# Two fp32 tiles instead of three in a fused attention and FFN kernel, with a new emission order

## The chip, the cores and the metric

One core of a Trainium2 chip runs the whole program. The metric is the device time of one execution in microseconds. A profiled execution gives the trace from which the rows below are read.

## The reference

Attention with rotary position embedding over 4 batches, 8 heads, 576 positions and head size 64, followed by a feed-forward network (FFN) without biases; both keep the accuracy of fp32.

```python
q_rot, k_rot = rotate(q), rotate(k)              # 4 x 8 x 576 x 64
scores = q_rot @ k_rot^T / sqrt(64)
attn = softmax(scores)
x = (attn @ v) as 2304 tokens x 512
h = x @ w_in                                     # 512 x 2048
g = h * clip(h + 3, 0, 6) / 6
out = g @ w_out                                  # 2048 x 512
```

The weights come as 64-bit floats and are decoded on the chip.

## The kernel before

The 2304 tokens are 18 tiles of 128. Attention works by head: 18 x 8 heads, numbered `i`, tile `t = i // 8`. Tiles 0 and 1 have an attention of their own in fp32 (`scores_first`, `attention_first`, `emit_first`), since nothing is ready yet; the others use fp16 halves: a value is a high fp16 part and a low fp16 part (`split_steps`), and a product is a sum of several fp16 products. For a later head, `attention(i)` runs the scores on TensorE (4 matmuls of 288 columns, L641), maximum and exponential on VectorE and ScalarE (L689, L692), the split of the result (L706, L710), a transposing DMA (L716), and the product with V on TensorE (14 matmuls of 64 columns, L659).

The FFN of a tile has four blocks of 512 hidden values. `ffn_h` makes `h`, `gate` the activation, `ffn_o` the output. The first `NF` (for `h`: `NH`) tiles, 0, 1 and 2, go in fp32: 64 matmuls of 128 columns (L994) and 16 of 512 columns (L1072). Each of them shows in the trace as two records. The other tiles take three fp16 products: 192 matmuls of 128 columns (L1005) and 48 of 512 columns (L1076). Their x is split in halves and transposed by DMA (`emit_x`, L942 to L950); that of tile 2 is transposed on TensorE (`emit_x32`, L906, through L356), as it is used in fp32. Their gate ends with a copy to fp16 and a subtraction (L1038 to L1040).

Each weight comes in eight pieces. `load_w` issues the loads on SyncE's queue, `decode_w` makes fp32 of them (ScalarE, then VectorE, L588), `bound_w` takes the largest absolute value (`wb` is its priority; `em.choose("wb" + kind, ...)` picks VectorE or ScalarE), `scale_w` makes one scale per weight when its eight bounds are there (`wscale`), and `split_w_steps` splits a piece in place into fp16 halves. It may do so when all fp32 tiles have used the piece (`used_h`, `used`), all 16 pieces are decoded and the scale is there.

The order of the instructions on every engine is the result of a small event simulation in the kernel (class `Emission`): a task is a generator that asks for an engine and a duration, has a priority, and is emitted when the modelled engine is free. `CFG` holds the priorities, and biases by which `choose` prices one engine against another for a kind of work: the key is the kind and the engine's letter (`wboD` is a bound of w_out on VectorE, `loD` a low half on VectorE, `hiP` a high half on GpSimd). There is a phase for the time until both scales are there, one until w_out is split, and a steady one after that; the first list of biases is that of the first phase. `lead` says how far attention may run ahead of the FFN.

Of the kernel before, what the change touches and what calls it, by code (L numbers as in the profile page):

```python
# [10 lines left out]
F16 = mybir.dt.float16  # L11
# [17 lines left out]
NG = 9  # L29
NP16 = 5  # L30
NR1 = 2
NF = 3
NH = 3
NQ = 1
NPT = 4


CFG = {'a0': -1.043, 'a1': -3.605, 'a2': 0.974, 'k1': -29.702, 'kv': 1.769, 'q1': 7.56, 'q': -6.449, 'wi': 8.789, 'wo': 8.272, 'gate': -5.153, 'x': -17.664, 'lead': 16, 'lat': 0.008, 'dma': 2.513, 'back': 0.938, 'a16': -1, 'v0': 1.625, 'wb': 8.917, 'si': 39.868, 'so': 46.239, 'bias': [{'loD': -32.8, 'elD': -3.19, 'glD': -43.45, 'ehD': 9.44, 'ghD': -8.07, 'ropeD': 22.52, 'xhD': -22.31, 'xlD': 3.83, 'hiP': -12.11, 'ehP': -11.5, 'ghP': 46.76, 'xhP': -6.78, 'lowP': 43.5, 'sgP': 45.86, 'hiD': -5.54, 'wboD': -25.15, 'qbD': 19.8, 'biD': -12.43, 'lowD': 31.78, 'sgD': 25.7, 'mxA': 35.95, 'wbiD': -40.0}, {'loD': -6.35, 'elD': 32.31, 'glD': 28.97, 'ehD': 2.19, 'ghD': 20.72, 'ropeD': -5.14, 'xhD': 15.28, 'xlD': 10.72, 'hiP': 46.71, 'ehP': 35.11, 'ghP': -0.16, 'xhP': -16.14, 'lowP': -7.78, 'sgP': 5.66, 'hiD': 14.24, 'wboD': 17.36, 'qbD': 17.86, 'biD': 17.27, 'lowD': 27.25, 'sgD': 34.77, 'mxA': 49.38, 'wbiD': -45.6}, {'loD': -12.12, 'elD': -8.64, 'glD': 11.8, 'ehD': 6.42, 'ghD': 1.59, 'ropeD': 4.05, 'xhD': -14.03, 'xlD': -21.15, 'hiP': 29.79, 'ehP': -7.99, 'ghP': -38.73, 'xhP': -6.56, 'lowP': 12.34, 'sgP': -25.71, 'hiD': 7.07, 'wboD': -25.64, 'qbD': 13.79, 'biD': 3.66, 'mxA': 56.44, 'wbiD': -44.43}], 'kvs': 4, 'vpos': 1, 'q0': 'DP', 'ch': 9.975, 'ks': 4.636, 'h': 9.28, 'r1': 'P', 'late': 2.97, 'r1n': 8, 'steady': {'x': -16.457, 'lead': 36, 'a2': -1.508, 'gate': -14.915, 'kv': 21.843, 'q': -15.069, 'dma': 0.74}, 'swap': -99.0}


class Emission:
# [36 lines left out]
    def free(self, name):  # L78
        self.tokens[name] += 1
# [31 lines left out]
    def step(self, gen, prio, end, prev, sent=None):  # L111

        try:
            e, x = gen.send(sent)
        except StopIteration:
            return
        if prev == "E" and e != "E":
            end += 0.17
        go = lambda t, p=None, s=None: self.post(t, lambda: self.step(gen, prio, t, p, s))
        if e == "N":  # L120
            go(end, prev)
        elif e == "U":
            go(end + x)
        elif e == "T":
            if x["done"]:
                go(end)
            else:
                x["then"].append(lambda t: self.step(gen, prio, max(t, end), None))
        elif e in "SZ":
            self.post(end + 0.05, lambda: self.dma(x, e, lambda t: self.step(gen, prio, t + (CFG["steady"] if self.phase == 2 else CFG)["dma"], None)))  # L130
        elif e == "C":
            self.post(end, lambda: self.poll(x, gen, prio, None))
        elif e == "R":
            def take():
# [27 lines left out]
    def choose(self, kind, x, prio):  # L162

        def cost(e):
            E = e.upper()
            ahead = max(self.busy[E] - self.clock, 0.0) + sum(w[2] for w in self.waiting[E] if w[0] <= prio)
            if e in "dP":
                ahead = max(ahead, self.port - self.clock - self.PORT[E])
            return ahead + x[e] + CFG["bias"][self.phase].get(kind + E, 0.0)
        return min(x, key=cost)  # L170

    def dispatch(self, e):
# [17 lines left out]
def attention_ffn(ctx: ExitStack, tc, q, k, v, w_in, w_out, rope, ident, out):  # L190
# [10 lines left out]
    em = Emission({"S": 2, "P16": NP16, "PT": NPT, "av": 1, "x": 1, "h": 2, "tg": 2, "g": NG,  # L201
                   "o": 1, "ob": 1, "rope": 1, "rope0": 1, "k16": 1, "raw": 3, "raw1": NR1, "tw": 2, "rope1": 1})
    free, when, spawn = em.free, em.when, em.spawn
    cfg = lambda k: (CFG["steady"] if em.phase == 2 else CFG)[k]

    left = ctx.enter_context(tc.tile_pool(name="left", bufs=1))
    psum = ctx.enter_context(tc.tile_pool(name="psum", bufs=1, space=bass.MemoryType.PSUM))
# [64 lines left out]
    tw_free = [0, 1]  # L272
# [101 lines left out]
    def prep_q(t, raw):  # L374

        x, at = raw
        yield "T", at
        am = col("qam", 1, 2)
        e = yield "Xqb", {"D": 0.675, "A": 0.72}
        q1 = left.tile([128, 8, 2, 64], F16, tag="q16", bufs=2, name="q1")  # L380
        bound(e, am, x, q1.rearrange("p h a d -> p (h a d)")[:, 0:512])
        yield "D", 0.54
        p2 = pow2_rows(am, "qp2", 2, 2.0 ** -14)
        s = col("qs", 1, 2)
        DVE.reciprocal(out=s, in_=p2)
# [12 lines left out]
        SP.dma_start_transpose(out=qT[:, 1], in_=q2.rearrange("p h a d -> p (h a d)"))
        yield "P", 0.65
        pk = p2k[b0] if b0 == b1 else mixcol(p2k[b0], p2k[b1], f"pkm{t}")  # L400
        sg = col("sig", 2, 3)
        POOL.tensor_tensor(out=sg[:, 0:1], in0=p2, in1=pk, op=ALU.mult)
        POOL.tensor_scalar(out=sg[:, 1:2], in0=sg[:, 0:1], scalar1=2.0 ** -17, scalar2=None, op0=ALU.mult)
        POOL.tensor_scalar(out=sg[:, 0:1], in0=sg[:, 0:1], scalar1=-2.0 ** -17, scalar2=None, op0=ALU.mult)
        sig_t[t] = sg
        yield "N", 0.0
        if em.phase == 2:
            yield "U", CFG["late"]
        qT_t[t] = qT


# [151 lines left out]
    def decode_w(kind, i, raw, at, token):  # L563

        yield "T", at

        yield "C", lambda: kind == "i" or len(k32_in) == 5 and 0 in qT_t

        yield "C", lambda: kind == "i" or i < 6 or len(tw) == 4
        c = stage(kind, i)  # L570

        yield "A", 1.15
        ACT.activation(out=c, in_=raw[:, :, 1].bitcast(F32), func=ACTF.Prelu, scale=2.0 ** -112, alpha=-2.0 ** 32)
        yield "R", "tw"
# [12 lines left out]
        yield "d", 1.21
        DVE.scalar_tensor_tensor(out=cu, in0=cu, scalar=3, in1=low,  # L588
                                 op0=ALU.logical_shift_left, op1=ALU.bitwise_or)
        yield "N", 0.0  # L590
        decoded[kind].add(i)

        def give():
            tw_free.append(n)
            free("tw")

        spawn(bound_w(kind, i, t, give), CFG["wb"])
        spawn(split_w_steps(kind, i), CFG["s" + kind] + i / 1000)

    def bound_w(kind, i, t, give):  # L600
        c = stage(kind, i)
        e = em.choose("wb" + kind, {"D": 1.21, "A": 1.16}, 3)
        if e == "D":
            give()
        yield e, 1.21 if e == "D" else 1.16
        bound(e, wam[kind][:, i:i + 1], c, t.bitcast(F16)[:, 0:1024])
        yield "N", 0.0
        if e == "A":
            give()
        bounded[kind].add(i)  # L610

    def split_w_steps(kind, i):

        yield "C", lambda: min(used_h, default=8) > i - 2 if kind == "i" else min(used, default=8) > i
        yield "C", lambda: decs() == 16 and kind in wscale and set(range(i - 1 if kind == "i" else i)) <= split_w[kind]
        if kind == "i":
            c, hi, lo = stage(kind, i), wi_h(i, 0), wi_h(i, 1)
        else:
# [51 lines left out]
    def attention(i):  # L670
# [462 lines left out]
    kv = []  # L1133
# [103 lines left out]
```

## Time and profile before

| | us |
|---|---|
| median of 3 runs | 606.47 |
| lowest, highest | 606.04, 609.99 |
| the profiled execution | 608.99 |
| its span | 607.1 |
| TensorE busy | 576.2 |
| VectorE busy | 457.6 |
| ScalarE busy | 354.5 |
| GpSimd busy | 290.6 |

The profile calls TensorE's matmuls PE and its weight loads PEld, VectorE DVE, ScalarE ACT, GpSimd POOL and SyncE's queue SPq. L12 is line 12 of the kernel. A matmul is drawn from its start to the end of its result, so that successive ones overlap; the step from one start to the next is what it costs in a stream. The granted TensorE clock is the full 2.4 GHz nearly throughout (0.996 of it as a mean).

### The profile page before, as it was taken

What the parts mean: (1) busy time and instruction counts of PE and PEld (TensorE: products, weight loads), DVE (VectorE), ACT (ScalarE), POOL (GpSimd) and SP (SyncE); (2) the same over time, 40 slices, a digit from 0 to 9 for tenths busy, and PEclk for the clock granted to TensorE, in tenths of its full rate; (3) what the DMA queues carried; (4) which work ended last, traced back from release to release, by engine and by line L of the source; (5) the groups of instructions that cost most, each with busy time, mean ns of one, the idle gap of its engine ahead of it and who ended that gap; (6) DMA issues with size and microseconds to landing.
All of it is one profiled execution on the core that took longest, in us unless ns stands there. A gap on an engine that the chain in (4) does not pass through costs nothing.

```text
span 607.1 us, 17399 instructions
## 1 busy us (share of the span) xinstructions
PE 576.2 (95%) x7153; PEld 437.6 (72%) x7153; DVE 457.6 (75%) x850; ACT 354.5 (58%) x660; POOL 290.6 (48%) x373
## 2 busy tenths in 40 slices
PE   3888999999999998999999999999999999999996
PEld 2667777767667776787777777867677778777785
DVE  5998999996999985689588859877794877742131
ACT  5797875346777655476556545847564756541111
POOL 5540685423226995446299744545153643223200
PEclk9998999999999999999999999999999999999999
DMA  8989991996669969888986899899969798760000
GB/s 300 304 275 295 277 231 52 143 171 175 123 134 185 140 124 159 207 130 161 183 175 139 156 169 198 148 160 159 149 108 170 129 151 146 135 105 18 19 18 18
DMA packets 240287, 94.71 MB, mean 156 GB/s; under 512 B 222160, under 2 KB 224592, under 8 KB 240208
## 3 DMA queue, kind: packets, MB, share of 16 engines
q1 hardware_dynamic: 240208, 93.60, 76.8%
q8 instruction: 56, 0.92, 0.6%
q14 instruction: 23, 0.19, 0.1%
HBM read 31.97 MB, written 4.72 MB: 60 GB/s over the span
## 4 chain that ended last, share of the span: by engine, by line
PE 60%; DVE 15%; POOL 12%; DMA 6%; issue 5%; ACT 2%; SPq 0%; DVEq 0%; ACTq 0%; POOLq 0%
PE h L1005 17%; PE o L1076 17%; PE o L1072 6%; PE av L659 6%; PE S L641 5%; PE h L994 4%; POOL kst L316 3%; POOL ropeA L313 3%; DVE S L689 2%; POOL kst L318 2%; DMA wi_st<-x 2%; DMA PT<-P 2%; DVE P L710 2%; PE S L644 2%; POOL g L1040 1%
## 5 line engine op out<-in xcount | busy, mean ns | idle before, releaser
L1005 PEld LDWEIGHTS <-wi_st 128*128 128x128 f16 x2880 | 176.1, 98 | 41.9 <-issue 2.7
L1076 PE MATMUL o<-wo_st,g 128*128 128x512 f16 (+1 forms) x636 | 161.5, 367 | 3.7 <-POOL g L1040 2.0
L692 ACT ACTIVATE S<-S,mx 128x576 f32<-128x576 f32 x128 | 91.4, 714 | 114.3 <-DVE S L689 101.9
L689 DVE TENSOR_SCALAR_CACHE_REDUCE S<-S,sig 128x576 f32<-128x576 f32 x128 | 103.4, 819 | 20.1 <-PE S L641 19.2
L1005 PE MATMUL h<-wi_st 128*128 128x128 f16 x1728 | 116.8, 219 | 1.2 <-DMA wi_st<-x 1.2
L710 DVE SCALAR_TENSOR_TENSOR P<-S,P 128x576 f16<-128x576 f32 x128 | 95.1, 753 | 27.8 <-ACT P L706 27.3
L330 POOL TENSOR_SCALAR g<-tg 128x512 f16<-128x512 f32 x45 | 29.2, 649 | 153.5 <-DVE tg L1029 147.7
L1022 ACT ACTIVATE tg<-h,g,block_sc 128x512 f32<-128x512 f32 x64 | 49.7, 776 | 65.5 <-PE h L1005 61.9
L1029 DVE SCALAR_TENSOR_TENSOR tg<-tg,h 128x512 f32<-128x512 f32 x60 | 41.0, 684 | 57.0 <-ACT tg L1022 56.9
L706 ACT ACTIVATE P<-S 128x576 f16<-128x576 f32 x128 | 81.7, 649 | 2.4 <-DMA PT<-P 0.3
L659 PEld LDWEIGHTS <-PT 128*128 128x128 f16 (+1 forms) x2016 | 67.4, 101 | 17.4 <-issue 5.5
L1076 PEld LDWEIGHTS <-g 128*128 128x128 f16 x636 | 54.5, 98 | 31.7 <-issue 3.0
L1005 PE MATMUL h<-xTa,wi_st 128*128 128x128 f16 x1152 | 77.1, 219 | 0.0
L659 PE MATMUL av<-vA,PT 128*128 128x64 f16 (+1 forms) x2016 | 73.0, 194 | 1.0 <-DMA PT<-P 0.6
L641 PE MATMUL S<-kT,qT 128*128 128x288 f16 x448 | 71.2, 286 | 2.1 <-DVE P L710 1.8
L1040 POOL TENSOR_TENSOR g<-tg,g 128x512 f16<-128x512 f32 x47 | 57.9, 1233 | 2.9
L994 PEld LDWEIGHTS h<-xTa,wi_st 128*128 128x128 f32 x384 | 48.1, 192 | 13.7 <-issue 12.8
L641 PEld LDWEIGHTS <-qT 128*128 128x128 f16 x448 | 39.5, 98 | 18.5 <-issue 5.0
L1072 PE MATMUL o<-wo_st,g 128*128 128x512 f32 x96 | 51.0, 613 | 0.7 <-DVE wo_st L588 0.7
L994 PE MATMUL h<-xTa,wi_st 128*128 128x128 f32 x384 | 49.2, 275 | 0.0
L313 POOL TENSOR_TENSOR ropeA<-qraw,rope_sb 128x512 f32<-128x512 f32 x17 | 23.8, 1401 | 33.5 <-DMA qraw<-in_q 33.4
L1076 PE MATMUL o<-wo_st 128*128 128x512 f16 (+1 forms) x132 | 32.4, 360 | 1.4 <-DVE wo_st L328 1.1
(151 smaller groups left out, 760.6 us busy)
## 6 DMA issues: line engine op xcount, KB each, us to landing
raw<-in_w_in SPq DMA_DIRECT2D x16, 512.0 KB, 6.6
raw<-in_w_out SPq DMA_DIRECT2D x16, 512.0 KB, 5.7
qraw<-in_q SPq DMA_DIRECT2D x18, 256.0 KB, 3.8
kst<-in_k SPq DMA_DIRECT2D x16, 256.0 KB, 4.8
vst<-in_v SPq DMA_DIRECT2D x15, 256.0 KB, 4.7
out<-wo_st SPq DMA_DIRECT2D x14, 256.0 KB, 3.5
PT<-P SPq DMA_TRANSPOSE x128, 3.4
vA<-vA SPq DMA_DIRECT2D x8, 256.0 KB, 4.2
```

What stands on the lines that cost most here:

```text
L641: PE.matmul(out=S[:, j, 0:288], lhsT=qT_t[t][:, o, h, :], rhs=kT_t[b0][:, h, ks], **st)
L659: PE.matmul(out=av[r0:r1, h, :], lhsT=PT[:, blk, r0:r1], rhs=rhs, start=(n == 0), stop=(n == len(terms) - 1))
L689: DVE.tensor_scalar(out=E, in0=E, scalar1=sig_t[t][:, 0:1], scalar2=3.0e38, op0=ALU.mult, op1=ALU.min, accum_out=mx)
L692: ACT.activation(out=E, in_=E, func=ACTF.Exp, scale=-1.0, bias=mx, accum_out=sum_t[t][:, h:h + 1])
L706: ACT.activation(out=hi, in_=E, func=ACTF.Copy, scale=ES)
L710: DVE.scalar_tensor_tensor(out=lo, in0=E, scalar=ES, in1=hi, op0=ALU.mult, op1=ALU.subtract)
L994: PE.matmul(out=h[:, i, :], lhsT=wi_st[:, p + 2, 256 * c + f0:256 * c + f0 + 128], rhs=xT[:, c, :], start=(c == 0), stop=(c == 3))
L1005: PE.matmul(out=h[:, i, :], lhsT=wi_h(p, wl)[:, 256 * c + f0:256 * c + f0 + 128], rhs=xT[:, 4 * xl + c, :], start=(n == 0), stop=(n == 11))
L1022: ACT.activation(out=tg, in_=hf, func=ACTF.Relu, scale=osc[j], bias=g3)
L1040: ENG[e].tensor_tensor(out=gf[:, 1], in0=tg, in1=gf[:, 0], op=ALU.subtract)
L1072: PE.matmul(out=os[n][0], lhsT=g[:, mm % nm, 128 * n:128 * n + 128], rhs=wo_st[:, mm + 2], start=(mm == 0), stop=(mm == 15))
L1076: PE.matmul(out=os[n][0][:, to], lhsT=g[:, gl, mm % nm, 128 * n:128 * n + 128], rhs=wo_h(mm, wl)[:, cs], start=(mm == 0 and gl == 0 and wl ...
```

## The change

Tile 2 goes through the FFN in fp16 halves like the later ones (`NF` and `NH` from 3 to 2). The planner's constants are new throughout. In the steady phase there are four sets of them, with biases of their own, chosen by the number of heads that are done (`PARTS`: up to 64, 88, 112 and above). Only two pieces of w_in, not all eight, are loaded into the two early buffers (`r1n`), the others into the three of w_out, and the pool of the FFN's tiles takes the place of the early buffers as soon as these are free. A bound on ScalarE takes a scratch tile of its own in place of keeping that of the decoding. The split of a piece waits for the scales of both weights.

```diff
-NF = 3
-NH = 3
+NF = 2
+NH = 2
+PARTS = 64, 88, 112
-CFG = {... 'wi': 8.789, 'wo': 8.272, 'lead': 16, 'wb': 8.917, 'bias': [{... 'wboD': -25.15, ... 'wbiD': -40.0}, ...
+CFG = {... 'wi': 10.746, 'wo': 3.955, 'lead': 22, 'wb': 12.863, 'bias': [{... 'wboD': 39.4, ... 'wbiD': -1.83}, ...
-  'vpos': 1, ... 'r1n': 8, 'steady': {'x': -16.457, 'lead': 36, ...}, 'swap': -99.0}
+  'vpos': 3, ... 'r1n': 2, 'steady': [{'x': -11.166, 'lead': 38, ... 'bias': {...}}, {... 'lead': 22, ...}, {... 'lead': 16, ...}, {... 'lead': 28, ...}], 'swap': -77.644, 'wbn': 1}
...
-            return ahead + x[e] + CFG["bias"][self.phase].get(kind + E, 0.0)
+            return ahead + x[e] + self.bias().get(kind + E, 0.0)
...
-    cfg = lambda k: (CFG["steady"] if em.phase == 2 else CFG)[k]
+    em.now = lambda: CFG["steady"][bisect.bisect_right(PARTS, len(done_av))] if em.phase == 2 else CFG
+    em.bias = lambda: em.now()["bias"] if em.phase == 2 else CFG["bias"][em.phase]
+    cfg = lambda k: em.now()[k]
...
-        spawn(bound_w(kind, i, t, give), CFG["wb"])
+        tw_free.append(n)
+        free("tw")
+        spawn(bound_w(kind, i), CFG["wb"])
         spawn(split_w_steps(kind, i), CFG["s" + kind] + i / 1000)
...
+    def bound_w(kind, i):
+        yield "C", lambda: decs() >= CFG["wbn"]
+        c = stage(kind, i)
+        e = em.choose("wb" + kind, {"D": 1.21, "A": 1.16}, 3)
+        if e == "A":
+            yield "R", "tw"
+            n = tw_free.pop()
...
-        yield "C", lambda: decs() == 16 and kind in wscale and set(range(i - 1 if kind == "i" else i)) <= split_w[kind]
+        yield "C", lambda: decs() == 16 and len(wscale) == 2 and set(range(i - 1 if kind == "i" else i)) <= split_w[kind]
```

The two waits of the steady phase that were `CFG["late"]`, and the model's delay behind a DMA, are taken from the set of the part.

## Rows read from the trace of the kernel before

**Rows 1.** The page's head and part 1: busy us, share, instructions.
```profile
span 607.1 us, 17399 instructions
PE 576.2 (95%) x7153; PEld 437.6 (72%) x7153; DVE 457.6 (75%) x850; ACT 354.5 (58%) x660; POOL 290.6 (48%) x373
```

**Rows 2.** By stretch: length, busy us (instructions) PE, PEld, DVE, ACT, POOL, clock, DMA, GB/s.
```profile
0.00:50.00 50.00, 32.56 (x265) 24.75 (x266) 43.09 (x70) 36.86 (x66) 22.42 (x24) 0.99 0.98 294
50.00:200.00 150.00, 147.91 (x1500) 110.23 (x1499) 137.58 (x235) 100.83 (x172) 68.83 (x80) 0.99 0.79 174
200.00:550.00 350.00, 344.34 (x4798) 262.24 (x4794) 265.54 (x530) 207.34 (x410) 188.73 (x258) 1.00 0.86 151
...
100.00:130.00 30.00, 29.58 (x292) 21.58 (x292) 29.60 (x55) 12.75 (x28) 10.95 (x16) 1.00 0.85 156
130.00:175.00 45.00, 45.00 (x357) 31.10 (x354) 37.17 (x64) 29.76 (x49) 8.22 (x13) 1.00 0.63 140
```

**Rows 3.** TensorE's timeline from 301 us: start, length, line, matmuls.
```profile
301.39 0.57 PE L659 MATMUL av<-vA,PT 128*128 128x64 f16 x14
301.80 0.65 PE L641 MATMUL S<-kT,qT 128*128 128x288 f16 x4
302.29 0.81 PE L1076 MATMUL o<-wo_st,g 128*128 128x512 f16 x3
302.94 0.83 PE L1005 MATMUL h<-wi_st 128*128 128x128 f16 x12
303.61 0.81 PE L1076 MATMUL o<-wo_st,g 128*128 128x512 f16 x3
```

**Rows 4.** The chain that ended last, in order of time: start, us, records.
```profile
54.86 0.89 PE h L994 x8
...
64.95 0.86 PE o L1072 x2
```

**Rows 5.** The page's groups, part 5: count, busy us, mean ns, idle before.
```profile
L1072 PE MATMUL o<-wo_st,g 128*128 128x512 f32 x96 | 51.0, 613 | 0.7 <-DVE wo_st L588 0.7
L994 PE MATMUL h<-xTa,wi_st 128*128 128x128 f32 x384 | 49.2, 275 | 0.0
```

**Rows 6.** Who waited for whom: us in total, times, longest us.
```profile
PE xt L356 <- DVE kst L318: 11.7, 3, 8.2
...
ACT wi_st L326 <- PE h L994: 8.7, 6, 2.4
...
DVE wi_st L338 <- ACT wi_st L326: 6.2, 4, 2.4
...
PE ET L776 <- ACT E L767: 3.9, 3, 2.1
```

**Rows 7.** Tile x, 100 to 160 us: ns min/median/max, first and last start.
```profile
L356 PE MATMUL xt<-id_sb,x x4: 272/272/273, 123.0 to 123.4; 128*128 128x128 f32 x4
...
L944 POOL TENSOR_TENSOR x<-x,x x1: 1701/1701/1701, 152.1 to 152.1; 128x512 f16<-128x512 f32 x1
L950 SPq DMA_TRANSPOSE xTa<-x x1: 1232/1232/1232, 153.8 to 153.8; - x1
```

**Rows 8.** The weights' tiles wi_st and wo_st, 0 to 200 us: bounds and splits.
```profile
L252 DVE TENSOR_REDUCE wami<-wi_st x8: 1200/1210/1215, 28.0 to 106.0; 128x1 f32<-128x1024 f32 x8
L338 DVE SCALAR_TENSOR_TENSOR wi_st<-wi_st,wsi x8: 1280/1283/1541, 128.0 to 169.3; 128x1024 f16<-128x1024 f32 x8
L326 ACT ACTIVATE wi_st<-wi_st,wsi x6: 1147/1148/1150, 136.0 to 155.5; 128x1024 f16<-128x1024 f32 x6
...
L252 DVE TENSOR_REDUCE wamo<-wo_st x8: 1202/1206/1219, 107.8 to 125.6; 128x1 f32<-128x1024 f32 x8
```

**Rows 9.** GpSimd's groups by line, 200 to 550 us.
```profile
L1040 POOL TENSOR_TENSOR g<-tg,g 128x512 f16<-128x512 f32 x38 | 45.5, 1196 | 2.2
```

**Rows 10.** Lines 994 and 1072 alone, 0 to 100 us: PE busy, PEld busy.
```profile
0.00:100.00 100.00, 22.07 (x177) 21.43 (x178) 0.98 0.90 255
...
0.00:100.00 100.00, 12.53 (x24) 3.66 (x24) 0.98 0.90 255
```

More of the change, by code (lines that the diff above doesn't have):

```diff
@@ L31 @@
 NR1 = 2
-NF = 3
-NH = 3
+NF = 2
+NH = 2
 NQ = 1
 NPT = 4
-CFG = {'a0': -1.043, 'a1': -3.605, 'a2': 0.974, 'k1': -29.702, 'kv': 1.769, 'q1': 7.56, 'q': -6.449, 'wi': 8.789, 'wo': 8.272, 'gate': -5.153, 'x': -17.664, 'lead': 16, 'lat': 0.008, 'dma': 2.513, 'back': 0.938, 'a16': -1, 'v0': 1.625, 'wb': 8.917, 'si': 39.868, 'so': 46.239, 'bias': [{'loD': -32.8, 'elD': -3.19, 'glD': -43.45, 'ehD': 9.44, 'ghD': -8.07, 'ropeD': 22.52, 'xhD': -22.31, 'xlD': 3.83, 'hiP': -12.11, 'ehP': -11.5, 'ghP': 46.76, 'xhP': -6.78, 'lowP': 43.5, 'sgP': 45.86, 'hiD': -5.54, 'wboD': -25.15, 'qbD': 19.8, 'biD': -12.43, 'lowD': 31.78, 'sgD': 25.7, 'mxA': 35.95, 'wbiD': -40.0}, {'loD': -6.35, 'elD': 32.31, 'glD': 28.97, 'ehD': 2.19, 'ghD': 20.72, 'ropeD': -5.14, 'xhD': 15.28, 'xlD': 10.72, 'hiP': 46.71, 'ehP': 35.11, 'ghP': -0.16, 'xhP': -16.14, 'lowP': -7.78, 'sgP': 5.66, 'hiD': 14.24, 'wboD': 17.36, 'qbD': 17.86, 'biD': 17.27, 'lowD': 27.25, 'sgD': 34.77, 'mxA': 49.38, 'wbiD': -45.6}, {'loD': -12.12, 'elD': -8.64, 'glD': 11.8, 'ehD': 6.42, 'ghD': 1.59, 'ropeD': 4.05, 'xhD': -14.03, 'xlD': -21.15, 'hiP': 29.79, 'ehP': -7.99, 'ghP': -38.73, 'xhP': -6.56, 'lowP': 12.34, 'sgP': -25.71, 'hiD': 7.07, 'wboD': -25.64, 'qbD': 13.79, 'biD': 3.66, 'mxA': 56.44, 'wbiD': -44.43}], 'kvs': 4, 'vpos': 1, 'q0': 'DP', 'ch': 9.975, 'ks': 4.636, 'h': 9.28, 'r1': 'P', 'late': 2.97, 'r1n': 8, 'steady': {'x': -16.457, 'lead': 36, 'a2': -1.508, 'gate': -14.915, 'kv': 21.843, 'q': -15.069, 'dma': 0.74}, 'swap': -99.0}
@@ new lines @@
+PARTS = 64, 88, 112
+CFG = {'a0': 1.618, 'a1': -0.363, 'a2': 2.411, 'k1': -39.456, 'kv': 10.07, 'q1': 6.898, 'q': -0.88, 'wi': 10.746, 'wo': 3.955, 'gate': -1.044, 'x': -25.343, 'lead': 22, 'lat': 0.008, 'dma': 2.666, 'back': 0.952, 'a16': -1, 'v0': 2.611, 'wb': 12.863, 'si': 37.306, 'so': 54.348, 'bias': [{'loD': -33.87, 'elD': 19.25, 'glD': -5.13, 'ehD': 43.87, 'ghD': 33.93, 'ropeD': 11.5, 'xhD': -11.72, 'xlD': -35.28, 'hiP': -18.84, 'ehP': -37.1, 'ghP': 37.1, 'xhP': -2.63, 'lowP': 51.2, 'sgP': 63.02, 'hiD': 46.92, 'wboD': 39.4, 'qbD': 0.77, 'biD': -46.05, 'lowD': 44.23, 'sgD': 8.72, 'mxA': 0.26, 'wbiD': -1.83}, {'loD': -1.79, 'elD': 36.87, 'glD': 20.17, 'ehD': 3.0, 'ghD': 13.26, 'ropeD': 44.72, 'xhD': 45.46, 'xlD': 11.61, 'hiP': 46.97, 'ehP': -39.02, 'ghP': 4.61, 'xhP': 5.04, 'lowP': 5.91, 'sgP': -43.07, 'hiD': 48.86, 'wboD': 36.09, 'qbD': 5.93, 'biD': 3.75, 'lowD': 58.05, 'sgD': 36.17, 'mxA': 21.9, 'wbiD': 1.12}], 'kvs': 4, 'vpos': 3, 'q0': 'DP', 'ch': 13.372, 'ks': 7.695, 'h': 6.754, 'r1': 'P', 'r1n': 2, 'steady': [{'x': -11.166, 'lead': 38, 'a2': -3.456, 'gate': -10.331, 'kv': 20.1, 'q': -20.107, 'dma': 0.91, 'late': 1.88, 'bias': {'loD': 2.81, 'elD': -9.43, 'glD': 42.05, 'ehD': 40.76, 'ghD': -10.69, 'ropeD': -43.38, 'xhD': -22.19, 'xlD': -6.27, 'hiP': 30.91, 'ehP': -34.19, 'ghP': -36.81, 'xhP': -17.15, 'lowP': 30.76, 'sgP': 37.25, 'hiD': 11.86, 'wboD': -4.89, 'qbD': 9.92, 'biD': 42.23, 'mxA': 29.42, 'wbiD': 1.63}}, {'x': -12.341, 'lead': 22, 'a2': 5.809, 'gate': -3.656, 'kv': 10.819, 'q': -10.617, 'dma': 0.95, 'late': 4.96, 'bias': {'loD': -6.39, 'elD': -9.27, 'glD': 8.7, 'ehD': 3.33, 'ghD': -4.74, 'ropeD': -47.87, 'xhD': -24.77, 'xlD': 4.3, 'hiP': 39.82, 'ehP': -31.21, 'ghP': -43.71, 'xhP': 41.72, 'lowP': 10.6, 'sgP': 3.87, 'hiD': 20.41, 'wboD': -40.27, 'qbD': 5.55, 'biD': 39.89, 'mxA': 7.73, 'wbiD': -0.99}}, {'x': -18.98, 'lead': 16, 'a2': 3.071, 'gate': -14.492, 'kv': 14.932, 'q': -13.462, 'dma': 0.65, 'late': 3.17, 'bias': {'loD': -7.51, 'elD': -8.9, 'glD': 2.9, 'ehD': 43.96, 'ghD': -3.32, 'ropeD': -41.26, 'xhD': -24.77, 'xlD': -15.43, 'hiP': 30.06, 'ehP': -15.76, 'ghP': -43.88, 'xhP': 5.81, 'lowP': 5.07, 'sgP': -20.61, 'hiD': 16.99, 'wboD': 3.21, 'qbD': 9.77, 'biD': -5.07, 'mxA': 34.99, 'wbiD': -9.87}}, {'x': -12.862, 'lead': 28, 'a2': -4.147, 'gate': -11.172, 'kv': 18.371, 'q': -11.809, 'dma': 0.91, 'late': 2.23, 'bias': {'loD': 0.49, 'elD': -1.06, 'glD': 5.94, 'ehD': 6.06, 'ghD': -4.91, 'ropeD': -40.45, 'xhD': -23.95, 'xlD': 41.76, 'hiP': 30.3, 'ehP': -3.73, 'ghP': -41.57, 'xhP': -11.77, 'lowP': 7.95, 'sgP': -16.99, 'hiD': -4.88, 'wboD': -3.22, 'qbD': 1.23, 'biD': 40.44, 'mxA': 1.87, 'wbiD': 55.95}}], 'swap': -77.644, 'wbn': 1}
@@ L129, in step @@
         elif e in "SZ":
-            self.post(end + 0.05, lambda: self.dma(x, e, lambda t: self.step(gen, prio, t + (CFG["steady"] if self.phase == 2 else CFG)["dma"], None)))
+            self.post(end + 0.05, lambda: self.dma(x, e, lambda t: self.step(gen, prio, t + self.now()["dma"], None)))
         elif e == "C":
@@ L407, in prep_q @@
         if em.phase == 2:
-            yield "U", CFG["late"]
+            yield "U", cfg("late")
         qT_t[t] = qT
@@ L591, in decode_w @@
         decoded[kind].add(i)
-        def give():
+        tw_free.append(n)
+        free("tw")
+        spawn(bound_w(kind, i), CFG["wb"])
+        spawn(split_w_steps(kind, i), CFG["s" + kind] + i / 1000)
+    def bound_w(kind, i):
[5 more added lines that the diff above has]
+            n = tw_free.pop()
+        yield e, 1.21 if e == "D" else 1.16
+        bound(e, wam[kind][:, i:i + 1], c, tw[n].bitcast(F16)[:, 0:1024] if e == "A" else None)
+        yield "N", 0.0
+        if e == "A":
             tw_free.append(n)
             free("tw")
-        spawn(bound_w(kind, i, t, give), CFG["wb"])
[L598 to L609, printed above, removed]
         bounded[kind].add(i)
@@ L719, in attention @@
         if em.phase == 2:
-            yield "U", CFG["late"]
+            yield "U", cfg("late")
         if h == 0:
```

## The prediction, made before the change was run

> **What bounds the kernel now.** I read the busy shares first. TensorE is busy 576.2 of 607.1 us; the next engine, VectorE, 457.6 [rows 1]. The table by stretch says where the other 31 us of TensorE lie [rows 2]: 50 - 32.6 = 17.4 us before 50 us, 2.1 us between 50 and 200, 5.7 us between 200 and 550, and the last 5.7 us at the end. A busy TensorE can hide pauses, since each matmul is drawn longer than the step to the next, so I looked at the starts in the timeline of a steady stretch [rows 3]: 14 matmuls of attention times V take 0.41 us to the next start, 4 matmuls of scores 0.49, 3 of the second FFN product 0.65, 12 of the first 0.67. Those steps recur without holes. So after 50 us TensorE's matmuls are the bound, and a microsecond of matmul taken out is a microsecond of time, as long as the other engines keep delivering.
>
> Before 50 us it is another regime: VectorE has 43.1 of 50 us busy [rows 2], and TensorE's longest waits are for what VectorE and ScalarE make of the first keys and scores [rows 6]. From 100 to 130 us VectorE has 29.6 of 30 us too, with TensorE full beside it [rows 2]. These two places are where the change can go wrong.
>
> **The change part by part.** *Tile 2 leaves the fp32 route.* An fp32 product shows as two matmul records. The first FFN product has 384 such records for three tiles, the second 96 [rows 5], so a tile has 128 and 32. 8 of the former take 0.89 us and 2 of the latter 0.86 us where they run undisturbed [rows 4]: 16 x 0.89 = 14.2 us and 16 x 0.86 = 13.8 us, 28.0 us a tile. In fp16 the tile costs 16 x 0.67 = 10.7 us and 16 x 0.65 = 10.4 us [rows 3], 21.1 us. Saved: 6.9 us. The four TensorE transposes of its x go as well (start 123.0 to 123.4, some 0.5 us with the last one's step [rows 7]). TensorE's matmuls shrink by 7.4 us.
>
> The Trainium skill, "TensorE: Matmul & The Clock Gate", section "Back-to-back issue gap", says against this that a stream of weight-load and matmul pairs sustains only about 81 ns a matmul at 128 columns and 131 ns at 512. An estimate by that page: 192 x 81 = 15.6 us and 48 x 131 = 6.3 us, so the first product would lose 1.4 us by the change, the second would win 7.5, and 6.1 us would be left in place of 6.9. The trace shows 12 in 0.67 us, 56 ns each, and 3 in 0.65, 217 ns each [rows 3], so the sum goes by the rows.
>
> *What tile 2 adds elsewhere.* It now goes the way of the later tiles: its x is split in two fp16 halves, the subtraction 1.70 us on GpSimd where the trace shows it, and goes through a transposing DMA, 1.23 us of SyncE's queue [rows 7]; its four gate blocks each gain a copy to fp16 and a subtraction, on GpSimd 1.20 us for the latter [rows 9]. With the copies taken at half a subtraction (bounds: nothing, if ScalarE takes them, and as long as the subtraction) this is 4 x 1.8 + 1.7 + 0.6, some 9.5 us of GpSimd. GpSimd works 8.2 us of the 45 between 130 and 175 [rows 2], so that hides; on VectorE, which has 37.2 of 45, it would not quite.
>
> *The weights' split.* An fp16 product needs the weights split into halves, in place, and a piece may be split only after every fp32 tile has used it. Now that means tiles 0 and 1. In the trace this gate costs VectorE's work: the subtractions run from 128.0 to 169.3 us, ScalarE's copies wait 8.7 us for tile 2's matmuls and VectorE 6.2 us for those copies [rows 6, 8]. That wait goes. But a new one comes: a piece of w_in now waits for the scale of w_out too. Before, the bounds of w_out ran on VectorE between 107.8 and 125.6 [rows 8]. Behind that stand all splits, and behind them the whole fp16 FFN. The new biases of the early part price w_out's bounds on VectorE 39 up where they were 25 down, so they should go to ScalarE, which is busy 12.8 of 30 us there [rows 2]; a pass of the same 1024 columns takes 1.15 us on it [rows 8]. So both scales come somewhere between 108 us (just behind the last bounds of w_in at 106.0) and 127 (as now). I take 112.
>
> *Does TensorE have work until then?* Up to 100 us before ran 177 and 24 of the fp32 records [rows 10]. Of the two tiles' 256 and 64, 79 and 40 are left: 79 x 0.89/8 + 40 x 0.43 = 8.8 + 17.2 = 26.0 us. A head of attention is 0.41 + 0.49 = 0.9 us [rows 3]; tile 3 and the products with V of tile 2, 7.2 + 3.3 us, are at hand: an estimate of 36 us, until about 136. From the first split piece (one ScalarE and one VectorE pass, 1.15 + 1.28 us [rows 8]) tile 2's first product runs. So there is no hole unless the scales come 20 us after my value. From there each piece of either weight opens 1.3 us of matmul per tile. VectorE must now put all 16 x 1.28 = 20.5 us of splits beside attention. From 100 to 175 it has 8.2 us idle [rows 2], and gets back 8 x 1.21 = 9.7 us if w_out's bounds leave it: 17.9 us, against 8 x 1.28 = 10.2 us of w_out's splits pulled into this stretch. It fits, with little room; that tight fit costs between 0 and 8 us of TensorE waits, and I take 1.
>
> *The order anew.* Loads of w_in use two early buffers for two pieces in place of eight, and three others after that. The DMA engines are busy 0.98 of the first 50 us [rows 2], so arrival in total cannot come sooner; I take nothing, within 1 us either way, covered by the decoding. The FFN's pool opens sooner by the same change, but the first product ran only at 54.7 us, behind tile 0's attention; nothing. Two of w_in's bounds, 1.21 us each from 28.0 us on [rows 8], lose the bias that held them on VectorE in the stretch where VectorE is the bound: if both go to ScalarE, 2.4 us. I take 2.4; the bound on the other side is a loss of 3, if the new priorities delay the first scores by one 1.2 us pass at two or three places. The four parts of the late stretch can win at most its idle 5.7 us [rows 2], and a worse order can lose as much; VectorE and GpSimd have room there (busy 265.5 and 188.7 of 350). I take nothing.
>
> *Sum.* -6.9 - 0.5 + 1 - 2.4 = -8.8 us. The profiled execution spans 607.1 and took 608.99 us, 1.9 us around the span that stay; it lies 2.5 us above the median shown, 606.47. The span becomes 598.3, the profiled time some 600.2; taken from the median, 597.7. I say 597.5.
>
> **The rivals.**
>
> *VectorE becomes the bound from 100 to 200 us.* For it: 137.6 of 150 us busy between 50 and 200 [rows 2], and the same splits in less time. Against it: GpSimd and ScalarE are free there, and 14.9 us of chained waits go [rows 6]. The upper bound of my tight fit then holds, 8 in place of 1: 604.5. 0.17.
>
> *The pace is not TensorE's.* Then the 7.4 us do not come back, and only the early 2.4 do, less the 1: 605. Against it are the steps without holes [rows 3]. The Trainium skill, "Perfetto Trace Analysis", section "Identifying the Most-Contended Engine", has weight-load busy time, not matmul busy time, as TensorE's measure. That is 437.6 us, 72% [rows 1], which would leave TensorE room. The rows' steps speak against that rule here. 0.06.
>
> *TensorE runs dry after 136 us, slower.* The new gate waits for w_out's scale; if those bounds stay on VectorE at their low priority, or the pieces follow each other slowly, TensorE spends its 36 us and then goes at the pace of the splits. 16 pieces open 16 x 1.3 = 21 us of tile 2 and as much of tile 3, 42 us. With the scales at 127 and 9 us in stock, 51 us of work are there: a piece every 3.2 us just keeps up, and the time is lost from there: at 4.4 us apiece 70 us pass for 51 of work, 19 us lost, 597.5 - 1 + 19 = 615.5. It decides above 612.5 from 4.2 us apiece. For it: now w_in's pieces come 5.9 us apart, (169.3 - 128.0)/7 [rows 8]. Against it: that pace is tile 2's own fp32 gate. 0.09.
>
> *The waits go too.* The early stretch gains 6 instead of 2.4 us, and the late one half of its 5.7, 2.9: 591. 0.08.
>
> **How the numbers follow.** The forecast 597.5 has 0.60; its own range is 593.5 to 603: down by the 1 us of the tight fit and half of the late 5.7, up by 5.4 if the early stretch loses 3 where I have 2.4 won. The measurement can tell about 1%, 6.1 us, from no change: below 600.4 is faster, above 612.5 slower. Of the forecast 0.53 is below 600.4 and 0.07 above; with the last rival faster has 0.61, within 1% 0.07 + 0.17 + 0.06 = 0.30, slower 0.09. For 8 in 10 I go from 590.5 to 605.
>
> **What the profile after would show.** TensorE busy near 569 us; 256 and 64 fp32 records; the 128-column fp16 records up by 192 and the 512-column ones by 48. No four transposes of x. Splits of w_in starting near 112 us, w_out's bounds on ScalarE, no waits of ScalarE on the fp32 product. TensorE full from 50 us on. I am wrong if TensorE shows holes between 110 and 200 us that end on a split (VectorE or dry TensorE: the releaser tells which, a subtraction or a scale), or if the first 50 us have more than 17.4 us idle, or if the late stretch has waits beyond 5.7 us.

## The result and the profile after

The changed kernel takes 598.22 us (median of 4 runs, 597.56 to 598.60), the kernel before 606.80 beside it: 8.6 us or 1.4% less. The ratio on record, which is taken over the single runs and not over the medians, is 0.9847, with a 95% interval of 0.9827 to 0.9867. The forecast was 597.5, its range 590.5 to 605. Measured again later, the two took 598.14 and 608.08, a ratio of 0.983 (0.9799 to 0.9862). Two single executions that took about twice as long as the others of their kernel (1188.89 us of the kernel before, beside e1, and 1487.98 us of e11) are left out of all numbers.

The page of the changed kernel, head and part 1, beside [rows 1]:

```profile
span 596.6 us, 17620 instructions
PE 567.3 (95%) x7241; PEld 432.9 (73%) x7241; DVE 432.7 (73%) x817; ACT 374.7 (63%) x704; POOL 319.4 (54%) x397
```

By stretch, columns as in [rows 2]: length, then busy us (instructions) of PE, PEld, DVE, ACT and POOL, clock, DMA share, GB/s.

```profile
0.00:50.00 50.00, 33.41 (x265) 25.80 (x267) 42.78 (x68) 39.97 (x72) 22.49 (x24) 1.00 0.92 298
50.00:200.00 150.00, 145.06 (x1638) 107.51 (x1635) 138.22 (x235) 117.73 (x209) 85.98 (x89) 1.00 0.86 180
200.00:550.00 350.00, 346.50 (x4870) 266.46 (x4868) 242.36 (x501) 209.35 (x414) 204.25 (x278) 1.00 0.82 149
...
100.00:130.00 30.00, 29.95 (x298) 22.38 (x296) 27.92 (x44) 22.32 (x37) 12.62 (x16) 1.00 0.87 159
130.00:175.00 45.00, 44.58 (x664) 33.32 (x663) 41.15 (x73) 35.52 (x64) 19.80 (x20) 1.00 0.79 153
...
550.00:596.60 46.60, 42.38 (x481) 33.16 (x478) 9.29 (x15) 7.70 (x11) 6.70 (x8) 0.99 0.05 18
```

TensorE is busy 8.9 us less. Its idle time is 16.6 us before 50 us (17.4 before), 4.9 between 50 and 200 (2.1), 3.5 between 200 and 550 (5.7) and 4.2 at the end (5.7), 1.6 us less in all. The two sum to the 10.5 us by which the profiled span is shorter. That is more than the 8.6 us of the medians, since the profiled execution of the kernel before lies 2.2 us above its median (608.99 against 606.80), and that of the changed kernel 0.1 (598.35 against 598.22).

VectorE works 25 us less, ScalarE and GpSimd 20 and 29 us more (13 of GpSimd's came with tile 2 alone, in e1). Of VectorE's 25 us, 23 lie between 200 and 550 us. Before 200 us it works as long as it did, 181.0 us against 180.7: w_out's bounds left it, and other work, two more splits among it, came in their place, while ScalarE works 20 us more there. This can be read in the weights' tiles (0 to 200 us: engine, operation, count, ns min/median/max, first and last start), beside [rows 8]. L255 and L257 are the bounds on VectorE and ScalarE. A split is a high half on ScalarE or GpSimd (L329, L333) and a low half, here on VectorE (L341):

```profile
L341 DVE SCALAR_TENSOR_TENSOR wi_st<-wi_st,wsi x8: 1269/1280/2290, 107.9 to 132.7; 128x1024 f16<-128x1024 f32 x8
L255 DVE TENSOR_REDUCE wami<-wi_st x7: 1202/1206/1221, 18.3 to 56.8; 128x1 f32<-128x1024 f32 x7
L329 ACT ACTIVATE wi_st<-wi_st,wsi x6: 1136/1146/1154, 109.4 to 129.2; 128x1024 f16<-128x1024 f32 x6
...
L333 POOL TENSOR_SCALAR wi_st<-wi_st,wsi x2: 1123/1336/1550, 99.5 to 100.6; 128x1024 f16<-128x1024 f32 x2
...
L257 ACT ACTIVATE wi_st<-wo_st x3: 1068/1069/1070, 82.2 to 97.8; 128x1024 f16<-128x1024 f32 x3
...
L341 DVE SCALAR_TENSOR_TENSOR wo_st<-wo_st,wso x8: 1272/1282/1465, 113.6 to 168.0; 128x1024 f16<-128x1024 f32 x8
...
L257 ACT ACTIVATE wo_st<-wo_st x5: 1042/1048/1073, 56.2 to 103.3; 128x1024 f16<-128x1024 f32 x5
```

w_out's eight bounds are on ScalarE (3 + 5 rows) and done at 104 us in place of 127. The timeline of VectorE has its scale, the last of the two, at 107.00:

```profile
107.00 0.15 DVE L247 TENSOR_SCALAR wso<-p2wo 128x1 uint32<-128x1 uint32 x1
```

On VectorE both weights' splits now run from 108 to 169 us; before, those of w_in alone ended at about 171.

### The profile page after: what moved, and what is told of

Read it like the earlier page. It is cut to its first block, busy times and chain, and to the rows that moved or that the text cites. A ratio compares the mean times of both kernels' runs of the same rounds, so it can differ in the third digit from the quotient of the medians.

```text
span 596.6 us, 17620 instructions
## 1 busy us (share of the span) xinstructions
PE 567.3 (95%) x7241; PEld 432.9 (73%) x7241; DVE 432.7 (73%) x817; ACT 374.7 (63%) x704; POOL 319.4 (54%) x397
## 4 chain that ended last, share of the span: by engine, by line
PE 56%; DVE 15%; ACT 10%; issue 8%; POOL 5%; DMA 4%; SPq 1%; DVEq 0%; ACTq 0%; POOLq 0%
PE o L1080 18%; PE h L1009 18%; PE av L663 6%; PE S L645 6%; PE o L1076 3%; DVE P L714 3%; DVE S L693 2%; ACT P L710 2%; PE h L998 2%; DMA PT<-P 2%; ACT S L696 2%; ACT tg L1026 1%; DMA raw<-in_w_out 1%; DMA qraw<-in_q 1%; DVE vam L255 1%
## 5 line engine op out<-in xcount | busy, mean ns | idle before, releaser
L1009 PEld LDWEIGHTS <-wi_st 128*128 128x128 f16 x3072 | 187.1, 98 | 40.5 <-issue 1.9
L696 ACT ACTIVATE S<-S,mx 128x576 f32<-128x576 f32 x123 | 87.7, 713 | 100.5 <-DVE S L693 92.0
L1009 PE MATMUL h<-wi_st 128*128 128x128 f16 x1920 | 129.1, 219 | 0.1
L693 DVE TENSOR_SCALAR_CACHE_REDUCE S<-S,sig 128x576 f32<-128x576 f32 x123 | 99.6, 820 | 23.4 <-PE S L645 19.1
L1033 DVE SCALAR_TENSOR_TENSOR tg<-tg,h 128x512 f32<-128x512 f32 x64 | 43.8, 684 | 62.2 <-ACT tg L1026 62.0
L333 POOL TENSOR_SCALAR g<-tg 128x512 f16<-128x512 f32 x41 | 25.9, 631 | 86.2 <-DVE tg L1033 75.7
L1080 PE MATMUL o<-wo_st 128*128 128x512 f16 (+1 forms) x180 | 45.3, 365 | 0.0
L998 PEld LDWEIGHTS h<-xTa,wi_st 128*128 128x128 f32 x256 | 31.7, 192 | 7.4 <-issue 6.7
L1076 PE MATMUL o<-wo_st,g 128*128 128x512 f32 x64 | 33.4, 608 | 0.0
L998 PE MATMUL h<-xTa,wi_st 128*128 128x128 f32 x256 | 32.6, 275 | 0.0
```

Source lines behind the costliest of these rows:

```text
L693: DVE.tensor_scalar(out=E, in0=E, scalar1=sig_t[t][:, 0:1], scalar2=3.0e38, op0=ALU.mult, op1=ALU.min, accum_out=mx)
L696: ACT.activation(out=E, in_=E, func=ACTF.Exp, scale=-1.0, bias=mx, accum_out=sum_t[t][:, h:h + 1])
L998: PE.matmul(out=h[:, i, :], lhsT=wi_st[:, p + 2, 256 * c + f0:256 * c + f0 + 128], rhs=xT[:, c, :], start=(c == 0), stop=(c == 3))
L1009: PE.matmul(out=h[:, i, :], lhsT=wi_h(p, wl)[:, 256 * c + f0:256 * c + f0 + 128], rhs=xT[:, 4 * xl + c, :], start=(n == 0), stop=(n == 11))
L1076: PE.matmul(out=os[n][0], lhsT=g[:, mm % nm, 128 * n:128 * n + 128], rhs=wo_st[:, mm + 2], start=(mm == 0), stop=(mm == 15))
L1080: PE.matmul(out=os[n][0][:, to], lhsT=g[:, gl, mm % nm, 128 * n:128 * n + 128], rhs=wo_h(mm, wl)[:, cs], start=(mm == 0 and gl == 0 and wl ...
```

## The experiments

All results in one table; a ratio is to the kernel before, run beside it. That kernel's own median was 606.8 to 608.6 us from one time to the next, so differences of 1 or 2 us between rows are read from the ratios.

| run | fp32 tiles | order | us | ratio (95%) |
|---|---|---|---|---|
| changed kernel | 2 | new | 598.22 | 0.9847 (0.9827 to 0.9867) |
| e5, the same again | 2 | new | 598.14 | 0.983 (0.9799 to 0.9862) |
| e1 | 2 | old | 610.24 | 1.0051 (1.0031 to 1.0071) |
| e2 | 3 | new | 617.09 | 1.0152 (1.0132 to 1.0172) |
| e3 | 2 | new early, old late | 604.67 | 0.9959 (0.9939 to 0.9978) |
| e4 | 2, 256 more matmuls | new | 619.08 | 1.0206 (1.0169 to 1.0243) |
| e6 | 2 | old, w_out's bounds on ScalarE | 609.22 | 1.001 (0.9985 to 1.0034) |
| e7 | 2 | new, w_out's bounds on VectorE | 612.66 | 1.0071 (1.0046 to 1.0097) |
| e8 | 2 | old early, new late | 617.56 | 1.0148 (1.0112 to 1.0184) |
| e9 | 2 | new, early constants jittered | 615.51 | 1.012 (1.0083 to 1.0156) |
| e10 | 2 | new, late constants jittered | 599.52 | 0.9848 (0.9817 to 0.9878) |
| e11 | 2 | new, one late set | 605.15 | 0.9955 (0.9936 to 0.9975) |
| e12 | 2 | searched again | 603.29 | 0.9921 (0.9893 to 0.995) |

**Two fp32 tiles alone (e1).** The theory: the smaller matmul work is the gain. The rival: the new order is.

```diff
 (the kernel before)
-NF = 3
-NH = 3
+NF = 2
+NH = 2
```

> The kernel before with two fp32 tiles in place of three and nothing else of the change: its constants, its one steady set, its loads and its gate on one scale stay. If the smaller matmul work is the gain and the old order can still feed TensorE, this takes 7.4 us off 606.8: 599.4, up to 605 if the weights' splits, which the old constants place late, leave holes between 110 and 200 us. If the new order is the gain, it takes 606 us or more, and the trace shows idle TensorE in place of the 28 us of fp32 work.

610.24 us: not faster, but 0.5% slower. The page shows both halves of it. TensorE's busy time fell from 576.2 to 569.1 us, 7.1 us, about the 7.4 of the sum; its idle time rose from 30.9 to 38.1, by 7.2. The stretches where that idle time lies (columns as above):

```profile
130.00:175.00 45.00, 37.79 (x597) 30.36 (x593) 44.04 (x66) 31.14 (x51) 25.98 (x31) 1.00 0.64 138
175.00:200.00 25.00, 21.03 (x250) 10.72 (x249) 22.88 (x45) 16.40 (x31) 7.58 (x12) 1.00 0.66 136
```

TensorE stands 7.2 + 4.0 = 11.2 us in these 70; before it stood 0.9, and in the changed kernel 4.0. VectorE has 44.0 of 45 us. TensorE's waits from 125 to 200 us (us in total, times, longest) name the weights' splits first, with 5.7 of the 11.2 us, and the timeline has the scale of w_out at 127.85 us:

```profile
PE o L1076 <- DVE wo_st L338: 4.2, 5, 1.4
PE h L1005 <- DVE tg L1029: 2.0, 1, 2.0
PE h L1005 <- DVE wi_st L338: 1.5, 1, 1.5
```

So the gain in matmuls is real, and in the old order it is lost, half of it in waits on the weights' splits. These are the signs of the first rival of the forecast, VectorE as the bound, and of the late scale of the third; e6 below tests whether the late scale is the cause.

**Three tiles in the new order (e2).**

```diff
 (the changed kernel)
-NF = 2
-NH = 2
+NF = 3
+NH = 3
```

> The changed kernel with three fp32 tiles, all new constants and the four steady sets kept. Matmul work as the gain: 598.2 + 7.4 = 605.6 us, TensorE busy some 575 us. The new order as the gain: 600 us or less. If the two hang together (the new constants fit only two tiles): over 610.

617.09 us, 18.9 above the changed kernel, of which 575.5 - 567.3 = 8.2 us are TensorE's busy time. The other half is idle time. This is the last case of the expectation: the constants fit two tiles. How much of the loss any order that was not searched for would have cost, e2 can't tell (see e9).

**More matmuls (e4).** This measures whether TensorE is the bound, apart from any weight.

```diff
                     n = 0
+                    PE.matmul(out=h[:, i, :], lhsT=wi_h(p, 0)[:, f0:f0 + 128], rhs=xT[:, 0, :], start=True, stop=True)
```

> The changed kernel with one more fp16 matmul of 128 columns ahead of each of the 256 groups of the first FFN product of tiles 2 to 17 (the group overwrites its result), and the planner told of 0.056 us each: 256 x 0.056 = 14.3 us more of TensorE work, nothing else. TensorE's matmuls as the bound: 598.2 + 14.3 = 612.5 us. If another engine sets the pace and TensorE's drawn busy time hides pauses, as the share of weight-load time (73%) would have it: under 603.

619.08 us, 20.9 more. The timeline of TensorE, with the added matmul in line 1007, shows what one costs in a stream:

```profile
304.42 0.22 PE L1007 MATMUL h<-wi_st 128*128 128x128 f16 x1
304.48 0.83 PE L1010 MATMUL h<-wi_st 128*128 128x128 f16 x12
305.14 0.81 PE L1081 MATMUL o<-wo_st,g 128*128 128x512 f16 x3
```

Some 0.06 us, and then the same step as without it: 256 times, 15 us. Nothing hides it. The profiled execution is 19.0 us longer than that of the changed kernel (615.6 against 596.6), so some 4 us more came with it; one place is the granted clock (last section). Of the 19.0 us, TensorE is drawn busy for 17.6 and idle for 1.4, and the other engines' instructions are those of the changed kernel but for one (817, 704 and 396 on VectorE, ScalarE and GpSimd), so hardly a choice of the planner moved. TensorE's work is the bound. The rule of the Trainium skill that the prediction weighed ("Perfetto Trace Analysis", section "Identifying the Most-Contended Engine") has weight-load busy time, beside the share of peak arithmetic, as the measure of TensorE's headroom. By weight-load time, 73% in the changed kernel, there would have been room; the measurement decides against that here.

**The late sets (e3, e11, e10).** e3 puts the single steady set of before in all four places; e11 the first of the new four; e10 moves every late constant by at most 1, as a control.

```diff
 (the changed kernel's CFG)
-'steady': [set 1, set 2, set 3, set 4]
+'steady': [set of before] * 4      # e3
+'steady': [set 1] * 4              # e11
```

> The changed kernel with the single steady set of before (its priorities and its biases) in place of the four. By my sum the late parts are worth nothing to 3 us: 598 to 601, with TensorE idle between 200 and 550 us rising from 3.5 to about 5.7. If the four parts carry the gain: 604 or more.

> The changed kernel with the first of its four steady sets for the whole late stretch. If parts of their own bring the late gain: 602 or more. If one set of new constants does as well and the third experiment only had a set that did not fit: 598 to 600.

> The same for the late stretch: each priority and bias of the four steady sets moved by at most 1, the early constants untouched. If the 6.5 us of the third experiment are what the four sets bring, this stays within 2 us of 598.1; if they are the price of any order that was not searched for, it takes 602 to 605.

604.67, 605.15 and 599.52 us. So either other late order costs 1.1 to 1.3% (0.9959 and 0.9955 against 0.983 to 0.985), some 6.5 us, where the sum had nothing. The control cost nothing that can be told from zero; it is a weak one, since its page has the changed kernel's counts of instructions on VectorE, ScalarE and GpSimd (817, 704, 397): moves of 1 changed few choices here. Whether the four sets bring the 6.5 us, or any late order that was not searched for behind this early part costs them, these runs do not show. The stretch from 200 to 550 us of e3 and then of e11:

```profile
200.00:550.00 350.00, 344.35 (x4824) 263.31 (x4822) 262.39 (x525) 205.01 (x406) 185.03 (x256) 1.00 0.84 150
```
```profile
200.00:550.00 350.00, 341.43 (x4787) 261.56 (x4785) 234.21 (x490) 219.58 (x437) 214.47 (x287) 1.00 0.85 150
```

The old set leaves 262 us on VectorE, the four sets 242, the first set alone 234. TensorE is idle 5.7, 3.5 and 8.6 us. Less on VectorE is thus not better in itself. In e11 TensorE waits longest there for the transposing DMA of P, 5.8 us in 7 waits (total, times, longest), where the changed kernel has one wait of 0.9:

```profile
PE av L663 <- DMA PT<-P: 5.8, 7, 1.5
```

Idle time does not show all of the cost. The profiled e3 is 5.7 us longer than the changed kernel (602.3 against 596.6). After 200 us TensorE is idle 3.0 us more, and drawn busy 2.7 us more.

**w_out's bounds (e6, e7).** If scale and bounds carry the early part, moving them in the old order should bring most of the gain, and moving them back in the new one should cost it.

```diff
-'bias': [{... 'wboD': -25.15, ...
+'bias': [{... 'wboD': 39.4, ...     # e6: e1's kernel
-'bias': [{... 'wboD': 39.4, ...
+'bias': [{... 'wboD': -90.0, ...    # e7: the changed kernel
```

> The kernel of the first experiment (old order, two fp32 tiles, 610.2 us) with one bias moved, that of w_out's bounds on VectorE in the early phase from -25.15 to +39.4, so that its eight bounds go to ScalarE. If the 7 us of matmuls were lost because w_out's scale came at 127.9 us and VectorE was full (44.0 of 45 us between 130 and 175), the scale now comes near 108 us, the 11 us of holes between 125 and 200 us shrink to some 4, and the time falls to 602 to 604. If the whole order has to be new for it: 608 or more.

> The changed kernel with the reverse: the bias of w_out's bounds on VectorE at -90 in the early phase, so that all eight run there. If bounds and scale carry the early part of the gain, they cost VectorE 9.7 us and delay both weights' splits: 602 to 606. If ScalarE was only another place for them: 600 or less.

e6: 609.22 us, the second case of the expectation; by the ratios it is 0.4% better than e1. The bounds went to ScalarE and the scales came early, at 109 and 113 us by the timeline, and no wait on a weight's split is left among TensorE's waits from 100 to 200 us. In their place stands another:

```profile
PE h L1005 <- DMA xTa<-x: 4.6, 1, 4.6
PE S L641 <- DVE P L710: 2.3, 1, 2.3
```

The tile's x was made at 156.8 us and its halves passed GpSimd at 157.5 and 159.3, so that the transpose went out at 160.5, when TensorE had been at the next FFN group since 159.0. The weights were no longer late; x was. The profiled execution is the longest of e6's ten (612.76 us, mean clock 0.986), so not all of its waits need be in the others. TensorE's idle time from 50 to 200 us is 9.3 us in it, against 12.5 in e1 and 4.9 in the changed kernel.

e7: 612.66 us, beyond both cases. The scale of w_out came at 117.4 us instead of 107.0 and TensorE's idle time between 130 and 200 us is 3.1 + 3.3 us against 4.0. That explains little of 14.5 us. The profiled execution is 13.4 us longer than the changed kernel's: TensorE is idle 2.2 us more before 50 us, 3.1 between 50 and 200, 4.4 between 200 and 550 and 1.1 at the end, and drawn busy 2.6 us more.

**The corner (e8) and the control (e9).**

```diff
 (the changed kernel's CFG)
-(early constants of the change)
+(early constants of before)                          # e8, with the gate on one scale
+(each early constant + a random amount of at most 1) # e9
```

> Two fp32 tiles, the early constants, loads and gate on one scale of before, and the four steady sets of the change: the fourth corner beside the first experiment (old early, old late, 610.2), the third (new early, old late, 604.7) and the changed kernel (598.2). If the two parts of the order add up, 610.2 - 6.5 = 603.7 us. If the late sets only pay where the early part delivers: 607 or more.

> A control for the edits of the order. The changed kernel with each priority and bias of the early phases moved by a random amount of at most 1 (they lie between -46 and 63), the steady sets untouched; no bound, split or load is meant to change its engine. If the costs of the seventh and eighth experiment (14.5 and 19 us above the changed kernel) are those of what they moved, this stays within 2 us of 598.1. If any untuned order costs as much, it takes 605 or more, and those costs can't be put down to bounds and scale alone.

e8 takes 617.56 us. The four corners with two fp32 tiles are 610.2 (old early, old late), 604.7 (new, old), 598.1 (new, new) and 617.6 (old, new). The late sets bring 6.5 us behind the early part that they belong to, and cost 7.4 behind the other. They do not add up. Of e8's 7.3 us in span over e1, 2.9 are idle time of TensorE before 200 us. The late sets begin when w_out is split, near 190 us, so they can hardly have cost these.

e9 takes 615.51 us, 17 more than the changed kernel, for random moves of at most 1. So the 14.5 and 19 us of e7 and e8 can't be put down to bounds and scale, as the expectation said. It is one draw, and not the clean control that was meant. w_out's bounds stayed on ScalarE, but all eight of w_in's are on VectorE now, and one low half of w_out's split went to GpSimd, for which TensorE then waited 1.8 us:

```profile
L255 DVE TENSOR_REDUCE wami<-wi_st x8: 1199/1204/1220, 18.8 to 65.1; 128x1 f32<-128x1024 f32 x8
L346 POOL TENSOR_TENSOR wo_st<-wo_st x1: 2568/2568/2568, 163.0 to 163.0; 128x1024 f16<-128x1024 f32 x1
```

Against the changed kernel TensorE is idle 6.3 us more between 50 and 200, and 8.5 more between 200 and 550, where the sets were not touched. The largest hole, on TensorE and VectorE (start, us, what):

```profile
105.12 5.75 DVE L341 SCALAR_TENSOR_TENSOR k<-kst,ks,k 128x512 f16<-128x512 f32 x1
110.79 0.15 DVE L238 TENSOR_REDUCE pm<-wamo 128x1 f32<-128x8 f32 x1
...
111.00 0.58 PE L242 MATMUL chain<-id_sb,pm 128*128 128x128 f32 x1 [4.80 <-DVE pm L238]
```

The scale's small matmul stands in TensorE's queue and waits 4.8 us for VectorE, whose reduction of the bounds stands behind the split of k; everything behind it on TensorE waits too. In an order that is fixed on every engine, one late instruction on VectorE held up TensorE as well.

**The order searched again (e12).** The changed kernel with all order constants moved by a random search on the kernel's own event model.

> The changed kernel, two fp32 tiles and all its code, with the whole set of constants searched again by small random steps until the planner's own event model ends 4.4 us sooner. If that model carries what makes an order good, it takes 594 us. If an order is good on the chip for things the model lacks (GpSimd and VectorE holding each other up, landing times of DMAs), the gain does not come and it takes 598 to 606, although it was searched for.

603.29 us: worse than the changed kernel by 5, better than the kernel before. So an order that the model ends 4.4 us sooner was not better on the chip; none of these runs beats the changed kernel. What the model lacks stays open. It does know one thing that the expectation names as missing: `dispatch` keeps VectorE and GpSimd apart by a shared `port`. How close that comes to the chip, no run tested.

## Why the prediction was right, and where only its sum was

**The bound and the matmul work: right.** The page after has 256 and 64 fp32 records, and the bound is shown by e4. TensorE's busy time fell 8.9 us against 7.4. Where only the tile changed, in e1, it fell 7.1, and GpSimd worked 13 us more (9.5 taken). About 1 us of the rest is the clock: the profiled execution of before had some 3 us at the lower clock level behind a pause (last section), which are drawn as busy.

```profile
L1076 PE MATMUL o<-wo_st,g 128*128 128x512 f32 x64 | 33.4, 608 | 0.0
L998 PE MATMUL h<-xTa,wi_st 128*128 128x128 f32 x256 | 32.6, 275 | 0.0
```

**The split and its gate: right in the main.** The last scale came at 107.0 us (112 taken, 108 to 127 as bounds), VectorE's splits followed from 107.9, w_out's bounds were on ScalarE, and no ScalarE pass waits for tile 2's matmuls. Two readings were off. The scale does not stand behind w_in's bounds, which end at 58 us now and not at 107; it stands behind the last of w_out's on ScalarE, at 104. And not all splits wait for it: GpSimd made the first two high halves of w_in from 99.5 us on (the row of L333 above), since the new gate is one of the planner, which sets the order of the instructions and is no wait on the chip. The tight fit cost 4.9 - 2.1 = 2.8 us of idle time from 50 to 200 us, inside the 0 to 8 of the sum; 1 was taken. In e1 the same stretch lost 12.5 - 2.1 = 10.4 us, so 8 was too small a bound for an order that does not fit. The holes that were named as the sign of being wrong did not come: of TensorE's waits between 100 and 200 us in the changed kernel none is on a split or a scale, and the two longest are

```profile
PE S L645 <- DVE P L714: 1.7, 2, 1.0
PE av L663 <- DVE x L941: 1.4, 1, 1.4
```

**The early stretch: wrong.** The sum had 2.4 us from two of w_in's bounds leaving VectorE. Seven of w_in's eight stayed there (the row of L255 above), with VectorE at 42.8 of 50 us; TensorE's idle time there fell 0.8. The bias had not gone, as the prediction has it; at -1.83 it still prices a bound on VectorE (1.21 us) below one on ScalarE (1.16 us), unless VectorE's queue is 1.8 us the longer one.

**The late stretch: wrong in size.** The sum took nothing, with 5.7 us of idle time as the most to be won. Idle time from 200 to 550 us fell by 2.2, and e3 and e11 put the value of the four sets at some 6.5 us against other sets. How much of this is a gain on the kernel before, whose one set went with its own early part, can't be told apart: in e8 the same four sets were worth nothing behind the old early part.

**The end.** The last stretch has 1.5 us less idle time, which no step foresaw.

The two errors, +1.6 us early and -2.2 late, nearly cancel; 1.8 and -1.5 more on the other two idle terms do as well. With -1.5 on the busy time the span fell by 10.5 us where the sum had 8.8; that the median, 8.6 us lower, meets it within 1 us is partly luck. The mechanism held for this one order. That matmul time taken out comes back as time is not true of the change of tile 2 as such: the same two tiles gained nothing in the old order (e1), and with one constant moved (e7) or all early ones jittered (e9) the new order lost more than the gain.

**The rivals.** VectorE as the bound between 100 and 200 us, and the splits behind the late scale, are what happens to the same two tiles in the old order (e1). They were avoided by the new one. What in the new order avoids it is open: it is not the place of w_out's bounds alone, since e6 moved just that and the hole came back behind x; and since the control e9 lost 17 us with w_out's bounds where they were, edits of single constants can't settle it. "The pace is not TensorE's" falls with e4. That the order is fragile, so that all three edits of its early constants (e7, e8, e9) cost 14 to 19 us and a whole set searched anew (e12) 5, stood nowhere in the prediction; it was the larger risk.

## What to carry to other kernels

Work taken from the bound engine is worth its time only if the engines that feed it keep up: here 7 us of matmuls were worth nothing in an order that was planned for three tiles, and came back in one made for two. Where the order on every engine is fixed beforehand, an edit and its re-planned order are one change; to credit a part of it, run a control with a meaningless jitter of the same constants. Price a re-planned order by a range on both sides as wide as such a jitter, not by the idle time that is left to win.

## What the runs showed of the hardware

**One VectorE instruction beside a queue of GpSimd ones.** The split of k in e9, with both operands in SBUF, takes 0.74 us where nothing disturbs it (at 107.1 us in the timeline of the kernel before), and 5.75 us here, from 105.12 on. GpSimd ran five instructions end to end in that time:

```profile
104.39 1.27 POOL L316 TENSOR_TENSOR ropeA<-qraw,rope_sb 128x512 f32<-128x512 f32 x1
105.65 1.11 POOL L333 TENSOR_SCALAR wi_st<-wi_st,wsi 128x1024 f16<-128x1024 f32 x1
106.74 1.25 POOL L319 TENSOR_TENSOR qraw<-qraw,rope_sb 128x512 f32<-128x512 f32 x1
107.98 1.11 POOL L333 TENSOR_SCALAR wi_st<-wi_st,wsi 128x1024 f16<-128x1024 f32 x1
109.07 1.25 POOL L321 TENSOR_TENSOR qraw<-qraw,ropeA 128x512 f32<-128x512 f32 x1
```

The last of them ends at 110.32, VectorE's 0.55 us later. The Trainium skill, "SBUF — State Buffer", section "Who interferes with whom", says that a VectorE instruction with two SBUF inputs contends with a GpSimd instruction that reads SBUF, and that the one that comes second blocks. The trace agrees, and goes further: if that is what held the split, VectorE did not get its turn between two GpSimd instructions, four times in a row. No run took GpSimd's instructions away to prove the cause.

**The granted clock behind a pause.** In the profile of before, TensorE waits 2.1 us for ScalarE, busy 0.70 of the 2 us from 48 to 50, and from 50 to 53 the granted clock is 0.52, about its lower level of 1.2 GHz; the changed kernel is busy 1.82 of those 2 us and keeps 1.00:

```profile
50.00:53.00 3.00, 3.00 (x18) 2.11 (x16) 1.40 (x3) 3.00 (x3) 0.28 (x1) 0.52 1.05 177
```
```profile
50.00:53.00 3.00, 2.88 (x34) 2.28 (x30) 2.96 (x5) 3.00 (x5) 0.00 (x0) 1.00 1.30 257
```

The same 12 score records (lines 747 and 751 of the two) take 2.36 us busy in the one stretch and 1.30 in the other: a pause of 2 us cost 1 us more behind it. In e4 the clock is 0.50 from 253 to 256 us, after TensorE had been busy 1.09 of the 3 us from 250 to 253.
